# Attention scores of a cached decode kernel: queries as weights in a zeroed block, transposed keys moving, exponentials turned back on TensorE

## Chip, core and metric

The kernel runs on one core of one Trainium2 chip. The metric is the device time of one execution in microseconds (us). An execution is profiled by the hardware profiler; other executions are timed without it.

The engines are called as the profile calls them: PE is the matrix engine, whose weight loads (PEld) overlap its matmuls; DVE, ACT and POOL are the vector, scalar and general engines; SP issues the transfers (DMA). Each engine takes its instructions in order. A matmul holds one operand in the array as weights (128 x 128) and streams the other, the moving one, through it column by column into PSUM.

## What is computed

Two decoder layers with shared weights, for 8 batch elements with one new token each. A layer is grouped attention over a cache of 8192 keys and values (32 query heads, 8 key/value heads, head size 128), then an MLP, each behind a layer norm and with a residual:

```python
def _A_ref(x, k_cache, v_cache, wq, wo):
    q = (x @ wq).reshape(B, Sq, Hq, Dh).transpose(0, 2, 1, 3)
    k = jnp.repeat(k_cache, rep, axis=1)
    v = jnp.repeat(v_cache, rep, axis=1)
    scores = jnp.einsum("bhqd,bhkd->bhqk", q, k) * (Dh ** -0.5)
    p = _softmax(scores, axis=-1)
    o = jnp.einsum("bhqk,bhkd->bhqd", p, v)
    return o.transpose(0, 2, 1, 3).reshape(B, Sq, Hq * Dh) @ wo

x = x + _A_ref(_layernorm(x), k_cache, v_cache, wq, wo)
x = x + _B_ref(_layernorm(x), w1, w2)          # silu(x @ w1) @ w2
x = x + _A_ref(_layernorm(x), k_cache, v_cache, wq, wo)
x = x + _B_ref(_layernorm(x), w1, w2)
```

Inputs are bf16. Both layers read the same caches, 2 MB of keys and 2 MB of values for each element and key/value head.

## The kernel before

**Tasks and positions.** A task is one layer, one element and one key/value head: 4 query heads against 8192 keys; there are 128. A task has 64 chunks of 128 keys, in 8 positions of 8 chunks (1024 keys, half a slot). The SBUF arena has 27 slots of 512 KB, each for a granule (16 chunks) of keys or values. `make_tasks` orders the tasks: for each element the five heads whose keys will be kept, then three heads of the second layer of the element before, three heads of the first layer of the next element, and then the second layer of the five kept heads. The last 18 of an element's 32 granules of keys stay in the arena, transposed, between the layers, so those tasks load almost only values.

**The loop (L616).** For each position `p` the instructions are recorded in this order:

- `emit_t_until(p + LT)`: PE transposes the 8 key chunks of position p + 3 against `ident` into one of three PSUM banks `TPp` (L387), and DVE or ACT copies them back over the keys (L395, L393).
- `emit_s(p)`: the scores (L418). Each chunk of 128 transposed keys is the weights, and 32 columns of queries (4 wanted, the rest overwritten by the next chunk or unused) move. The scores lie as 128 keys by 64 chunks x 4 heads in a PSUM bank `SCp`.
- `emit_pv(p - LP)`: the values of the position 12 earlier (L468), again with the chunk as weights, 4 columns of exponentials moving.
- At the first four positions after a task: `softmax_max` (DVE's reduce L427, POOL's all-reduce over the partitions L429), `softmax_exp` (DVE subtracts, L436; ACT's exp, L443), `softmax_sum` (DVE's reduce L448, POOL's all-reduce L451), `softmax_rcp` (L456).
- One step of an element's chain, if one is under way. A chain is what lies between the layers: output projection, layer norm in three steps (DVE, with POOL's all-reduces L492 and L507), up, silu, down, layer norm again, queries of the second layer; 11 steps, PE's matmuls being those of L536.
- `emit_norm` (L482) where the values of a task are done; after an element's last task of the first layer its chain begins.
- `issue_until(p)`: SP's loads that have a free slot.

**Order and waits.** The loads are planned ahead (`plan_loads`): the order is that of the positions at which they are needed, `LT` ahead of the scores for keys and `LP` behind for values, each into the slot that becomes free first. Each engine has one counting semaphore; `Sync` records for each tile who wrote and read it last and makes an instruction wait for these. At L619, before the first task of the second layer of an element, what is left of its chain is recorded in one go. When the tasks are done, the projection, norm and MLP of the second layer follow for all 8 elements at once.

Of the kernel before, what the change touches and what calls it, by code (L numbers as in the profile page):

```python
# [5 lines left out]
HQ = 32  # L6
# [6 lines left out]
GRP = 8  # L13
# [3 lines left out]
KEEP = 18  # L17
LT = 3
PRE = 10
LP = 12  # L20
SW = 32
NTP = 3
NSCP = 2
NP = 3
NST = 4
ACT_EVAC = (1, 4, 7)

BF16 = mybir.dt.bfloat16
# [160 lines left out]
def _build(ctx, nc, A_x, A_k_cache, A_v_cache, A_wq, A_wo, B_w1, B_w2, out):  # L189
# [39 lines left out]
    def chunk(slot, c):  # L229
        o = slot * SLOT + c * 128  # L230
        return ARENA[:, o:o + 128]
# [7 lines left out]
    w1_sb = sb([128, KT, F], BF16, "w1")  # L239
    w2_sb = sb([128, FT, D], BF16, "w2")  # L240
    ident = sb([128, 128], BF16, "ident")
    Xr = sb([128, D], BF16, "X")
    XT = [sb([128, KT, B], BF16, f"XT{n}") for n in range(3)]
    QPAD = SW - REP
    QT1 = sb([128, B * HQ + QPAD], BF16, "QT1")
    QT2 = [sb([128, HQ + QPAD], BF16, "QT2") for _ in range(2)]
    at1 = [sb([128, HQ], BF16, "at1") for _ in range(2)]
    at2 = sb([128, HQ, B], BF16, "at2")
    vr = sb([128, B], FP32, "vr")
# [6 lines left out]
    xnT = sb([128, KT, B], BF16, "xnT")  # L256
    eh = sb([128, FT * B], FP32, "eh")
    hsT = sb([128, FT * B], BF16, "hsT")
    SCs = sb([128, NCH * REP], FP32, "SCs")
    Ps = [sb([128, NCH * REP], BF16, "P") for _ in range(NP)]  # L260
    mxp = [sb([128, REP], FP32, "mxp") for _ in range(NST)]
    mxa = [sb([128, REP], FP32, "mxa") for _ in range(NST)]
    ssm = [sb([128, REP], FP32, "ssm") for _ in range(NST)]
    ssa = [sb([128, REP], FP32, "ssa") for _ in range(NST)]
    rcp = [sb([128, REP], FP32, "rcp") for _ in range(NST)]
# [60 lines left out]
    with nc.Block() as block:  # L326

        @block.sync
        def _(sync_eng):
            dma(sp, Xr[0:B, :], x_in, wsem["x"], writes=["X"])  # L330

            op(pool, lambda: pool.memset(ident[:, :], 1.0), writes=["ident"])
            op(
# [4 lines left out]
                ),  # L338
                reads=["ident"], writes=["ident"],
            )  # L340
            op(pool, lambda: pool.memset(QT1[:, B * HQ:], 0.0), writes=["QT1"])
            for n in range(2):
                op(pool, lambda n=n: pool.memset(QT2[n][:, HQ:], 0.0), writes=[f"QT2_{n}"])

            queue = list(loads)

# [19 lines left out]
            load_rest()  # L366

            evacs = [0]
            tnext = [0]

            def has_t(i):
# [7 lines left out]
            def emit_t(i):  # L379
                b, g, k, h = where(i)  # L380
                slot = k_slot[(b, g, k)]
                n = evacs[0]
                evacs[0] += 1
                tb = n % NTP
                tpv = TPp[tb][:, :].rearrange("p (k q) -> p k q", q=128)
                steps = [
                    lambda c=c: pe.transpose(tpv[:, c, :], chunk(slot, h * GRP + c), ident[:, :])  # L387
                    for c in range(GRP)
                ]
                mm_group(steps, reads=[r_half(slot, h), "ident"], writes=[f"TP{tb}"])  # L390
                dst = half(slot, h)
                if n % 8 in ACT_EVAC:
                    op(act, lambda: act.copy(dst, TPp[tb][:, :]), reads=[f"TP{tb}"], writes=[r_half(slot, h)])  # L393
                else:
                    op(dve, lambda: dve.tensor_copy(dst, TPp[tb][:, :]), reads=[f"TP{tb}"], writes=[r_half(slot, h)])  # L395

            def emit_t_until(i):
                while tnext[0] <= min(i, NG - 1):
                    if has_t(tnext[0]):
                        emit_t(tnext[0])  # L400
                    tnext[0] += 1

            def emit_s(i):
                ti = i // GPT
                layer, _b, _g = tasks[ti]
                b, g, k, h = where(i)
                slot = k_slot[(b, g, k)]
                if layer == 0:
                    q0, qt, rq = b * HQ + g * REP, QT1, "QT1"
                else:  # L410
                    q0, qt, rq = g * REP, QT2[b % 2], f"QT2_{b % 2}"
                rhs = qt[:, q0:q0 + SW]
                bank = ti % NSCP
                steps = []
                for c in range(GRP):
                    o = ((i % GPT) * GRP + c) * REP
                    steps.append(
                        lambda c=c, o=o: pe.matmul(  # L418
                            SCp[bank][:, o:o + SW], chunk(slot, h * GRP + c), rhs, start=True, stop=True,
                        )  # L420
                    )
                mm_group(steps, reads=[r_half(slot, h), rq], writes=[f"SC{bank}"])

            def softmax_max(ti):
                bank, st = ti % NSCP, ti % NST
                scv = SCp[bank][:, 0:NCH * REP].rearrange("p (c h) -> p h c", h=REP)
                op(dve, lambda: dve.tensor_reduce(mxp[st][:, :], scv, AX.X, ALU.max),  # L427
                   reads=[f"SC{bank}"], writes=[f"mxp{st}"])
                op(pool, lambda: pool.partition_all_reduce(mxa[st][:, :], mxp[st][:, :], 128, bass.bass_isa.ReduceOp.max),  # L429
                   reads=[f"mxp{st}"], writes=[f"mxa{st}"])  # L430

            def softmax_exp(ti):
                bank, st, pb = ti % NSCP, ti % NST, ti % NP
                op(
                    dve,
                    lambda: dve.tensor_tensor(  # L436
                        SCs[:, :].rearrange("p (c h) -> p c h", h=REP),
                        SCp[bank][:, 0:NCH * REP].rearrange("p (c h) -> p c h", h=REP),
                        mxa[st][:, :].unsqueeze(1).to_broadcast([128, NCH, REP]), ALU.subtract,
                    ),  # L440
                    reads=[f"SC{bank}", f"mxa{st}"], writes=["SCs"],
                )
                op(act, lambda: act.activation(Ps[pb][:, :], SCs[:, :], ACT.Exp, scale=SM_SCALE),  # L443
                   reads=["SCs"], writes=[f"P{pb}"])

            def softmax_sum(ti):
                st, pb = ti % NST, ti % NP
                op(dve, lambda: dve.tensor_reduce(  # L448
                    ssm[st][:, :], Ps[pb][:, :].rearrange("p (c h) -> p h c", h=REP), AX.X, ALU.add),
                   reads=[f"P{pb}"], writes=[f"ssm{st}"])  # L450
                op(pool, lambda: pool.partition_all_reduce(ssa[st][:, :], ssm[st][:, :], 128, bass.bass_isa.ReduceOp.add),  # L451
                   reads=[f"ssm{st}"], writes=[f"ssa{st}"])

            def softmax_rcp(ti):
                st = ti % NST
# [2 lines left out]
            def emit_pv(i):  # L458
                ti = i // GPT
                b, g, k, h = where(i)  # L460
                slot = v_slot[(b, g, k)]
                ob, pb = ti % 2, ti % NP
                otp = OTp[ob][:, 0:REP]
                steps = []
                for c in range(GRP):
                    cc = (i % GPT) * GRP + c
                    steps.append(
                        lambda c=c, cc=cc: pe.matmul(  # L468
                            otp, chunk(slot, h * GRP + c), Ps[pb][:, cc * REP:(cc + 1) * REP],
                            start=(cc == 0), stop=(cc == NCH - 1),  # L470
                        )
                    )
                mm_group(steps, reads=[r_half(slot, h), f"P{pb}"], writes=[f"OT{ob}"])

            def emit_norm(ti):
                layer, b, g = tasks[ti]
# [109 lines left out]
            def chain_of(b):  # L586
# [13 lines left out]
                    )  # L600
                    for kt in range(KT)
                ],
                reads=["X", "ident"], writes=["MISC"],
            )
            op(dve, lambda: dve.tensor_copy(XT[0][:, :, :], MISC[:, 0:KT * B].rearrange("p (k b) -> p k b", b=B)),
               reads=["MISC"], writes=["XT0"])
            for f in ln_stages(XT[0][:, :, :], "XT0", B):
                f()
            query(B, QT1[:, 0:B * HQ].rearrange("p (b h) -> p h b", h=HQ), "QT1")()

            chain = []
            chain_b = [None]
# [1 line left out]
            ntask = len(tasks)  # L614

            for p in range(NG + LP + GPT + 1):  # L616
                if p < NG:
                    layer, b, _g = tasks[p // GPT]
                    if layer == 1 and chain and chain_b[0] == b:  # L619
                        while chain:  # L620
                            chain.pop(0)()
                emit_t_until(p + LT)
                if p < NG:
                    emit_s(p)
                if 0 <= p - LP < NG:
                    emit_pv(p - LP)
                ti, ph = p // GPT - 1, p % GPT
                if 0 <= ti < ntask and ph < 4:
                    (softmax_max, softmax_exp, softmax_sum, softmax_rcp)[ph](ti)
                if chain:  # L630
                    chain.pop(0)()
                done = p - LP - GPT
                if done >= 0 and done % GPT == 0 and done // GPT < ntask:
                    tj = done // GPT
                    emit_norm(tj)
                    layer, b, _g = tasks[tj]
                    if layer == 0 and tj == last0[b]:
                        assert not chain
                        chain.extend(chain_of(b))
                        chain_b[0] = b  # L640
                issue_until(p)
# [13 lines left out]
                ],  # L655
                reads=["XT0", "ident"], writes=["MISC"],
            )
            op(dve, lambda: dve.tensor_copy(Xr[0:B, :], MISC[0:B, :]), reads=["MISC"], writes=["X"])
            syn.acquire(sp, reads=[res("X")])
            sp.dma_start(out_v, Xr[0:B, :]).then_inc(osem, 16)  # L660
            sp.wait_ge(osem, 16)

# [27 lines left out]
```

## Time and profile before

| what | us |
|---|---|
| median of 3 runs (1325.31 to 1330.08) | 1327.78 |
| the profiled execution's own span | 1321.8 |
| PE busy, matmuls / weight loads | 1009.8 / 983.4 |
| DVE / ACT / POOL busy | 545.3 / 328.8 / 117.8 |
| key transposes L387, 5888 of 128 x 128 | 564.0 |
| scores L418, 8192 of 128 x 32 | 394.2 |
| values L468, 8192 of 128 x 4 | 361.0 |
| all-reduces of the softmax, L429 / L451, 128 each | 47.7 / 55.2 |
| DVE's L427 / L436 / L448, ACT's L443, 128 each | 53.3 / 53.8 / 53.2, 53.4 |

The DMA engines moved 473.5 MB of inputs, a mean of 361 GB/s over the span. How to read it: matmuls overlap each other, so the busy times of PE are sums of overlapping spans, and the pace is read from the starts in the timeline. In a line of the timeline, the numbers are the start and the length in us; what stands in brackets at the end is the engine's idle time before the line and what ended it, "issue" being idle time for which the profile shows no cause. A line of windows gives, for each engine, the busy time and in brackets the instructions, then the granted clock of PE (1.00 is full), the busy share of the DMA engines and GB/s. The strip cuts the span in 40 slices of 33 us; its digits are tenths.

### The profile page before, as it was taken

How to read it: one execution, taken by the hardware profiler on the slowest of the kernel's cores; microseconds unless marked ns; L12 is line 12 of the kernel's file. 1: busy time of each engine (PE TensorE's matmuls, PEld its weight loads, DVE VectorE, ACT ScalarE, POOL GpSimd, SP SyncE). 2: the span in 40 equal slices, each digit the busy share in tenths (PEclk: the TensorE clock that was granted, in tenths of full speed). 3: DMA queues.
4: the chain of work that ended last, by engine and by line, in shares of the span. 5: the costliest groups of instructions: out<-in, count | busy, mean ns of one | idle time of the engine just before them, and what ended most of it. 6: DMA issues, size and time to landing. Idle time of an engine off the chain costs nothing.

```text
span 1321.8 us, 57028 instructions
## 1 busy us (share of the span) xinstructions
PE 1009.8 (76%) x25592; PEld 983.4 (74%) x25592; DVE 545.3 (41%) x1462; ACT 328.8 (25%) x414; POOL 117.8 (9%) x301
## 2 busy tenths in 40 slices
PE   3758867878677877778778886788867787788875
PEld 3757767877677877778778786787867787788874
DVE  2424434444343533444344442454434454344432
ACT  1323113312132222322123221331313222132210
POOL 0000010000000110000100001000010011000010
PEclk7878658858688776877678675886868867677765
DMA  8999899969999799997999889997999979999892
GB/s 342 386 399 403 291 371 408 377 230 398 408 407 376 256 407 407 408 344 286 408 408 395 303 344 407 408 383 275 377 408 407 388 243 407 407 406 357 287 408 112
DMA packets 133985, 477.14 MB, mean 361 GB/s; under 512 B 14176, under 2 KB 20080, under 8 KB 133232
## 3 DMA queue, kind: packets, MB, share of 16 engines
q1 hardware_dynamic: 133744, 473.51, 92.2%
q8 instruction: 203, 3.33, 1.0%
q14 instruction: 38, 0.31, 0.1%
HBM read 473.44 MB, written 0.01 MB: 358 GB/s over the span
## 4 chain that ended last, share of the span: by engine, by line
PE 53%; DMA 23%; issue 17%; DVE 5%; SPq 1%; POOL 1%; ACT 0%; POOLq 0%; DVEq 0%; ACTq 0%
PE TPp L387 24%; DMA arena<-in_A_k_cache_dram 18%; PE SCp L418 12%; PE OTp L468 11%; PE MISC L536 7%; DMA arena<-in_A_v_cache_dram 3%; SPq L301 1%; DVE arena L395 1%; DMA wq<-in_A_wq_dram 1%; DVE yr L522 1%; DVE tr L520 1%; DVE tr L519 1%; POOL s1a L507 0%; DVE xnT L524 0%; DVE yr L514 0%
## 5 line engine op out<-in xcount | busy, mean ns | idle before, releaser
L387 PE MATMUL TPp<-ident,arena 128*128 128x128 bf16 x5888 | 564.0, 253 | 109.2 <-DMA arena<-in_A_k_cache_dram 70.8
L387 PEld LDWEIGHTS TPp<-ident,arena 128*128 128x128 bf16 x5888 | 425.2, 113 | 117.4 <-DMA arena<-in_A_k_cache_dram 78.7
L395 DVE COPY arena<-TPp 128x1024 bf16<-128x1024 bf16 x460 | 317.3, 690 | 454.7 <-PE TPp L387 452.2
L393 ACT COPY arena<-TPp 128x1024 bf16<-128x1024 bf16 x276 | 278.6, 1010 | 688.6 <-PE TPp L387 688.6
L418 PE MATMUL SCp<-QT,arena 128*128 128x32 bf16 x8192 | 394.2, 184 | 68.6 <-issue 65.6
L468 PE MATMUL OTp<-P,arena 128*128 128x4 bf16 x8192 | 361.0, 165 | 79.3 <-issue 69.7
L418 PEld LDWEIGHTS SCp<-QT,arena 128*128 128x128 bf16 x8192 | 338.8, 103 | 71.0 <-issue 67.5
L468 PEld LDWEIGHTS OTp<-P,arena 128*128 128x128 bf16 x8192 | 290.7, 100 | 91.8 <-issue 81.0
L443 ACT ACTIVATE P<-SCs 128x256 bf16<-128x256 f32 x128 | 53.4, 417 | 271.4 <-DVE SCs L436 216.6
L429 POOL PARTITION_ALL_REDUCE mxa<-mxp x128 | 47.7, 373 | 727.0 <-DVE mxp L427 722.9
L451 POOL PARTITION_ALL_REDUCE ssa<-ssm x128 | 55.2, 431 | 296.4 <-DVE ssm L448 273.9
L427 DVE TENSOR_REDUCE mxp<-SCp 128x4 f32<-128x256 f32 x128 | 53.3, 417 | 46.5 <-PE SCp L418 46.5
L436 DVE TENSOR_TENSOR SCs<-SCp,mxa 128x256 f32<-128x256 f32 x128 | 53.8, 420 | 39.7 <-POOL mxa L429 39.7
L448 DVE TENSOR_REDUCE ssm<-P 128x4 f32<-128x256 bf16 x128 | 53.2, 416 | 41.2 <-ACT P L443 41.2
L536 PE MATMUL MISC<-xnT,wq 128*128 128x1 bf16 (+1 forms) x1152 | 31.8, 165 | 18.3 <-DVE xnT L524 18.2
L536 PEld LDWEIGHTS MISC<-xnT,wq 128*128 128x128 bf16 x1152 | 31.0, 102 | 19.1 <-DVE xnT L524 13.9
L482 DVE TENSOR_TENSOR at<-OTp,rcp 128x4 bf16<-128x4 f32 x128 | 20.0, 156 | 61.0 <-PE OTp L468 61.0
L536 PE MATMUL MISC<-at,wo 128*128 128x1 bf16 (+1 forms) x1152 | 32.5, 165 | 13.0 <-issue 12.7
L536 PEld LDWEIGHTS MISC<-at,wo 128*128 128x128 bf16 x1152 | 31.4, 101 | 13.7 <-issue 13.3
L456 DVE RECIPROCAL rcp<-ssa 128x4 f32<-128x4 f32 x128 | 22.0, 172 | 22.8 <-POOL ssa L451 22.8
L536 PE MATMUL MISC<-xnT,w 128*128 128x1 bf16 (+1 forms) x504 | 14.6, 165 | 18.4 <-DVE xnT L524 18.4
L536 PEld LDWEIGHTS MISC<-xnT,w 128*128 128x128 bf16 x504 | 13.9, 102 | 19.2 <-DVE xnT L524 17.2
(36 smaller groups left out, 111.2 us busy)
## 6 DMA issues: line engine op xcount, KB each, us to landing
arena<-in_A_v_cache_dram SPq DMA_DIRECT2D x512, 512.0 KB, 10.3
arena<-in_A_k_cache_dram SPq DMA_DIRECT2D x368, 512.0 KB, 12.2
wq<-in_A_wq_dram SPq DMA_DIRECT2D x2, 2048.0 KB, 9.4
wo<-in_A_wo_dram SPq DMA_DIRECT2D x1, 4096.0 KB, 26.0
w<-in_B_w_dram SPq DMA_DIRECT2D x2, 1792.0 KB, 22.6
X<-in_A_x_dram SPq DMA_DIRECT2D x1, 8.0 KB
out_dram<-X SPq DMA_DIRECT2D x1, 8.0 KB
```

The lines of the kernel that those rows point to most:

```text
L387: lambda c=c: pe.transpose(tpv[:, c, :], chunk(slot, h * GRP + c), ident[:, :])
L393: op(act, lambda: act.copy(dst, TPp[tb][:, :]), reads=[f"TP{tb}"], writes=[r_half(slot, h)])
L395: op(dve, lambda: dve.tensor_copy(dst, TPp[tb][:, :]), reads=[f"TP{tb}"], writes=[r_half(slot, h)])
L418: lambda c=c, o=o: pe.matmul(SCp[bank][:, o:o + SW], chunk(slot, h * GRP + c), rhs, start=True, stop=True,)
L427: op(dve, lambda: dve.tensor_reduce(mxp[st][:, :], scv, AX.X, ALU.max), reads=[f"SC{bank}"], writes=[f"mxp{st}"])
L429: op(pool, lambda: pool.partition_all_reduce(mxa[st][:, :], mxp[st][:, :], 128, bass.bass_isa.ReduceOp.max), reads=[f"mxp{st}"], writes=[f ...
L436: lambda: dve.tensor_tensor(SCs[:, :].rearrange("p (c h) -> p c h", h=REP), SCp[bank][:, 0:NCH * REP].rearrange("p (c h) -> p c h", h=REP) ...
L443: op(act, lambda: act.activation(Ps[pb][:, :], SCs[:, :], ACT.Exp, scale=SM_SCALE), reads=["SCs"], writes=[f"P{pb}"])
L448: op(dve, lambda: dve.tensor_reduce(ssm[st][:, :], Ps[pb][:, :].rearrange("p (c h) -> p h c", h=REP), AX.X, ALU.add), reads=[f"P{pb}"], wr ...
L451: op(pool, lambda: pool.partition_all_reduce(ssa[st][:, :], ssm[st][:, :], 128, bass.bass_isa.ReduceOp.add), reads=[f"ssm{st}"], writes=[f ...
L468: lambda c=c, cc=cc: pe.matmul(otp, chunk(slot, h * GRP + c), Ps[pb][:, cc * REP:(cc + 1) * REP], start=(cc == 0), stop=(cc == NCH - 1),)
L536: lambda o=o, k=k: pe.matmul(MISC[:, o * n:(o + 1) * n], w_sb[:, k, o * 128:(o + 1) * 128], rhs_of(k), start=(k == 0), stop=(k == kparts - 1),
```

## The change

The scores change sides. For each task, POOL copies its 4 query columns into a zeroed tile `QB` of 143 columns, 16 columns apart (`emit_q`). Of it, a 128-column slice that begins at 15 - j is the weights for key block j: query r then stands in column 16 r + j, and the other columns are zero. 512 transposed keys move at a time, 16 matmuls accumulate in one PSUM bank, and row 16 r + j gets the scores of head r against block j; 64 rows are used. The maximum per head becomes a reduce along the row and, across the rows of a head, two 32 x 32 transposes with a small reduce and a scaling on DVE; ACT's exp reads the scores from PSUM with that as its bias and sums each row; POOL multiplies a mask `hm` (which row belongs to which head) by these sums and adds over the partitions. PE turns the exponentials back, four transposes per task (`emit_pt`), DVE copies the 64 used columns to `PT`, and the values read columns of it 16 elements apart. The tiles for the input and the exponentials are one (`P`). Queries are copied three positions ahead, so a chain is recorded to its end three positions earlier, and the values lag 14 positions.

```diff
-LP = 12
-SW = 32
+LP = 14
-NP = 3
+NPT = 2
+NQB = 2
+KB = 512
...
+    NJ = NCH * 128 // KB
+    NR = NJ * REP
+    CPB = KB // 128
+    JPG = GRP * 128 // KB
+    QB = [sb([128, NJ - 1 + 128], BF16, "QB") for _ in range(NQB)]
...
+            def emit_q(ti):
+                layer, b, g = tasks[ti]
+                if layer == 0:
+                    q, rq = QT1[:, b * HQ + g * REP:b * HQ + (g + 1) * REP], "QT1"
+                else:
+                    q, rq = QT2[b % 2][:, g * REP:(g + 1) * REP], f"QT2_{b % 2}"
+                qb = QB[ti % NQB][:, 0:REP * NJ].rearrange("p (r j) -> p r j", j=NJ)[:, :, NJ - 1]
+                op(pool, lambda: pool.tensor_copy(qb, q), reads=[rq], writes=[f"QB{ti % NQB}"])
...
-                for c in range(GRP):
-                    o = ((i % GPT) * GRP + c) * REP
+                for c in range(JPG):
+                    j = (i % GPT) * JPG + c
                     steps.append(
-                        lambda c=c, o=o: pe.matmul(
-                            SCp[bank][:, o:o + SW], chunk(slot, h * GRP + c), rhs, start=True, stop=True,
+                        lambda c=c, j=j: pe.matmul(
+                            SCp[bank][:, :], QB[qn][:, NJ - 1 - j:NJ - 1 - j + 128], keys[:, c * KB:(c + 1) * KB],
+                            start=(j == 0), stop=(j == NJ - 1),
                         )
                     )
...
             def softmax_max(ti):
+                op(dve, lambda: dve.tensor_reduce(mxa[:, 0:1], SCp[bank][0:NR, :], AX.X, ALU.max),
+                   reads=[f"SC{bank}"], writes=["mxa"])
+                op(dve, lambda: dve.transpose(mxb[:, :], mxa[:, :]), reads=["mxa"], writes=["mxb"])
+                op(dve, lambda: dve.tensor_reduce(
+                    mxh[:, :], mxb[:, :].rearrange("p (r j) -> p r j", j=NJ), AX.X, ALU.max),
+                   reads=["mxb"], writes=["mxh"])
+                op(dve, lambda: dve.tensor_scalar(
+                    mxa[:, :].rearrange("p (r j) -> p r j", j=NJ),
+                    mxh[:, :].unsqueeze(2).to_broadcast([NR, 32 // NJ, NJ]), -SM_SCALE, None, op0=ALU.mult),
+                   reads=["mxh"], writes=["mxa"])
+                op(dve, lambda: dve.transpose(mxb[:, :], mxa[:, :]), reads=["mxa"], writes=["mxb"])
...
+                op(act, lambda: act.activation(
+                    P[0:NR, :], SCp[bank][0:NR, :], ACT.Exp, bias=mxb[:, 0:1], scale=SM_SCALE, accum_out=rs[st][:, :]),
+                   reads=[f"SC{bank}", "mxb"], writes=["P", f"rs{st}"])
 
             def softmax_sum(ti):
-                op(dve, lambda: dve.tensor_reduce(
-                    ssm[st][:, :], Ps[pb][:, :].rearrange("p (c h) -> p h c", h=REP), AX.X, ALU.add),
-                   reads=[f"P{pb}"], writes=[f"ssm{st}"])
+                op(pool, lambda: pool.tensor_scalar(
+                    ssm[st][0:NR, :], hm[:, :], rs[st][:, 0:1], None, op0=ALU.mult),
+                   reads=["hm", f"rs{st}"], writes=[f"ssm{st}"])
                 op(pool, lambda: pool.partition_all_reduce(ssa[st][:, :], ssm[st][:, :], 128, bass.bass_isa.ReduceOp.add),
                    reads=[f"ssm{st}"], writes=[f"ssa{st}"])
+
+            def emit_pt(ti):
+                pb = ti % NPT
+                tb = evacs[0] % NTP
+                evacs[0] += 1
+                tpv = TPp[tb][:, 0:KB].rearrange("p (c q) -> p c q", q=128)
+                steps = [
+                    lambda c=c: pe.transpose(tpv[:, c, :], P[:, c * 128:(c + 1) * 128], ident[:, :])
+                    for c in range(CPB)
+                ]
+                mm_group(steps, reads=["P", "Pz", "ident"], writes=[f"TP{tb}"])
+                op(dve, lambda: dve.tensor_copy(PT[pb][:, :, :], tpv[:, :, 0:NR]), reads=[f"TP{tb}"], writes=[f"PT{pb}"])
...
-                            otp, chunk(slot, h * GRP + c), Ps[pb][:, cc * REP:(cc + 1) * REP],
+                            otp, chunk(slot, h * GRP + c), pv[:, cc % CPB, cc // CPB, :],
...
+            LQ, LPT = 3, 4
+            emit_q(0)
...
-                if p < NG:
-                    layer, b, _g = tasks[p // GPT]
+                tq = (p + LQ) // GPT
+                if (p + LQ) % GPT == 0 and tq < ntask:
+                    layer, b, _g = tasks[tq]
                     if layer == 1 and chain and chain_b[0] == b:
                         while chain:
                             chain.pop(0)()
+                    emit_q(tq)
...
+                if 0 <= ti < ntask and ph == LPT:
+                    emit_pt(ti)
```

In the changed kernel POOL's multiply is line L472, its all-reduce L475 and its copy of the queries L431.

## The prediction

> **What bounds the kernel now.** I read the page's strip of 40 slices first, then the windows, then PE's and POOL's timelines. The strip:
>
> ```profile
> POOL 0000010000000110000100001000010011000010
> PEclk7878658858688776877678675886868867677765
> ...
> GB/s 342 386 399 403 291 371 408 377 230 398 408 407 376 256 407 407 408 344 286 408 408 395 303 344 407 408 383 275 377 408 407 388 243 407 407 406 357 287 408 112
> ...
> q8 instruction: 203, 3.33, 1.0%
> ```
>
> The caches arrive at a ceiling of 408 GB/s, with eight dips: 473.5 MB at 408 is 1160 us of 1321.8. Each dip is one element's chain (projection, layer norms, MLP, queries), whose steps PE takes in order between tasks. A window around one has 238 GB/s for 32 us (424 to 456), so 32 x (1 - 238/408) = 13 us are lost per chain, 8 x 13 = 107 in all; start and tail are the rest. POOL is nearly idle: 117.8 us, two all-reduces per task of 371 and 431 ns.
>
> A second limit lies close by. PE's weight loads in the tasks that keep their keys (timeline of that engine):
>
> ```profile
> 334.68 0.16 PEld L418 LDWEIGHTS SCp<-QT,arena 128*128 128x128 bf16 x3
> 337.62 0.21 PEld L418 LDWEIGHTS SCp<-QT,arena 128*128 128x128 bf16 x5 [2.78 <-issue]
> ...
> 341.24 0.10 PEld L418 LDWEIGHTS SCp<-QT,arena 128*128 128x128 bf16 x1
> 344.17 0.26 PEld L418 LDWEIGHTS SCp<-QT,arena 128*128 128x128 bf16 x7 [2.83 <-issue]
> ```
>
> PE stops 2.8 us every 6.5 us with nothing to wait for. 203 instruction transfers for 51,184 PE instructions are one per 252, and 203 x 6.4 is 1300 us: PE's instructions come hardly faster than it needs them.
>
> PE's clock halves and doubles between 3.41 us windows. Transposes (first count) in four of them:
>
> ```profile
> core 0: us, PE busy (x), PEclk, DMA share, GB/s
> 428.31:431.72 3.41, 2.61 (x23) 0.50 0.28 85
> 431.72:435.13 3.41, 0.30 (x5) 1.00 1.03 386
> 435.13:438.55 3.42, 2.03 (x16) 0.50 0.45 169
> 438.55:441.96 3.41, 1.41 (x13) 0.50 0.71 251
> ```
>
> With 24 score matmuls (32 columns) and 24 value ones (4) the first streams 23 x 128 + 768 + 96 = 3808 columns, and the next window has clock 1.00; the third, 16 x 128 + 512 + 64 = 2624, is followed by 0.50. In a chain PE seldom gets enough columns for full clock.
>
> **What decides.** POOL's timeline at the start:
>
> ```profile
> 0.78 0.20 POOL L332 MEMSET ident<- 128x128 bf16 x1 [0.29 <-POOLq L675]
> 9.19 0.28 POOL L335 TENSOR_SCALAR_AFFINE_SELECT ident<-ident 128x128 bf16<-128x128 bf16 x1 [8.20 <-issue]
> 9.44 0.11 POOL L341 MEMSET QT<- 128x28 bf16 x1
> 9.50 0.16 POOL L343 MEMSET QT<- 128x28 bf16 x2
> 25.86 0.43 POOL L492 PARTITION_ALL_REDUCE s1a<-s  x1 [16.20 <-DVE s L490]
> ```
>
> L335 needs only the memset that ended at 0.98, yet starts at 9.19: 8.20 us of "issue". In the list of the built program's instructions an unnamed entry stands just ahead of L335, and one ahead of the first all-reduce (L492), where its time, at most the 16.2 us before it, is covered by DVE's wait. After that POOL runs nothing but all-reduces, and no such entry comes. So it stands where POOL goes over to another family of operations: arithmetic to all-reduce or back. The changed program's list has it 256 times more, per task: entry, L472 multiply (hm x rs), entry, L475 all-reduce, then L431 copy into QB. I take both as what L335 paid, 8.2 us.
>
> [...]
>
> **The change, part by part.**
> - POOL per task: two entries 16.4, all-reduce 0.43, and multiply and copy some 0.2 each by the memset and select rows (0.11 to 0.28), with hops 1.0 for the three: 17.4 us against 10.3 us of DMA (4.19 MB at 408). The loop closes: the scores of task t+2 need QB, whose copy is queued on POOL behind the sum of task t, so PE can't run ahead. Queued behind that copy is the next entry, so POOL never rests; two QB buffers shift this and do not shorten it.
> - PE, scores: 64 matmuls of 32 columns per task become 16 of 512. Before, a position (one half slot) at full clock goes 202.23 transpose, 202.67 scores, 202.88 values, 203.08 next: 0.85 us, scores 0.21; at half clock 1.28 (428.59 to 429.87), scores 0.26. No 512-column matmul is in the trace. From below, 16 cost no more than 64 narrow ones (0.21 per position, were width free); from above, four times the mean transpose row (253 ns) is 1.0 us each, 2.0 per position. The transposes' pace (0.42 us for 8 x 128 columns, 0.85 at half clock) is nearest: 0.43 or 0.85 per position. With the transposes back (4 per task, 0.03) a position is 1.10 or 1.92, a task 8.8 or 15.4: under POOL's 17.4 either way, so worth nothing now. Without that cover it decides (rivals).
> - PE's instructions fall from 51,184 to 39,920, so some 158 transfers, 1030 us: that limit goes, behind POOL.
> - DVE: three 0.42 us operations go; a reduce over 512 (twice the 256 of L427, 0.8), four small ones at 0.16 and a copy of PT at 0.4 come: 1.8 against 1.25 us, on an engine 41% busy. ACT: exp over 512 instead of 256, from 0.42 to 0.6 between that row and the 1024-wide copy's 1.01. POOL's cycle covers both. DMA moves the same bytes.
> - Order: values two positions later, queries three earlier. LQ flushes the chain of the first and last element (24 positions to the first kept task, of which 14 and 11 steps are 25) with five steps in a row: a few us each, under POOL too. Each chain's four all-reduces need no entry but stand ahead of one, the second a position late: 1.9 + 0.7 (evacuation) + 0.4, so 3 us, 8 times: 24.
>
> **Sum.** Queries and the first two copies at 35 us (L536 ends at 33.8, then a 1.27 us cast). First scores and exp to some 47, entry, all-reduce and copy of task 2 at 57. 125 more cycles of 17.4: 2232. Sums of the last two tasks: 35. From the last normalisation to the end 17.2 as now (1304.62 to 1321.8), chains 24: 2308. The profiled execution spans 1321.8 and the runs shown have a median of 1327.78, 6 us more; so **2315 us**.
>
> [...] I stay at 8.2 for both: it is the one bare observation, taken at 309 GB/s (window 1 to 9), between a full DMA stream and the half-loaded one to come. A quarter less or more (6.2, 10.2) gives cycles of 13.4 and 21.4: 1800 and 2820.
>
> **Rivals.** From what price does POOL decide? 2 x entry + 1.0 must exceed 10.3: from 4.6 us on. Below, DMA's 1160 us stay and the eight chains decide.
> - *Entries cost little after the first; the clock stays low in chains: 1350.* For: L492's entry shows no cost of its own. [...] Some 14 positions per chain are exposed; a half-clock position streams about 2144 columns in 1.92 us, so 3800 in a window that nothing interrupts, near the bound, and a chain's matmuls interrupt. Half of the positions at 1.92 and part at 1.10 give 1.45 against 1.28: 2.4 us x 8 = 19, the two flushes 3 each: 1347 + 6, about 1350.
> - *The same, but wide scores hold the clock up: 1308, faster.* At full clock a window of 3.41 us has room for 3 positions, 6400 columns, and keeps well over 3808 with 1.3 us lost. If the chains then run at 1.10, 14 x 0.18 = 2.5 us are won per chain, 20 in all. It decides only with entries under 4.6 us, and if the two longest interruptions (3.5 us of projection, of queries) do not halve the clock for long.
> - *The change does not free PE:* a clock that ignores wide matmuls gives 15.4 us per task and under 2000; POOL hides that too.
>
> **Numbers.** Forecast 0.91, first rival 0.05, second 0.04 (the third is inside the forecast's range). The time is the forecast's, 2315; the range 1800 to 2820 is the entry's quarter each way, which leaves the rivals and an entry outside it, some 2 in 10, out. Over 0.3%, about what a measurement here tells from no change, faster: 0.04; within: 0.01; slower: 0.95.
>
> **What will show it.** POOL's timeline: some 8 us of "issue" ahead of each L472 and each L475, 17 us from one L431 copy to the next, always. PE waits for QB at the first scores of a task, DMA falls to some 205 GB/s (473.5 MB over 2310), and PE's 6.5 us stops vanish. Wrong it would be if L472 and L475 follow their inputs within a microsecond: then the GB/s strip returns to 408 with eight dips, and the clock in these decides.

## The result and the profile after

The changed kernel takes 2344.55 us (median of 4 runs, 2340.60 to 2358.54) against 1327.19 us for the kernel before: 1.7686 times as long, with a 95% interval of 1.7631 to 1.7741. The profiled execution spans 2338.9 us. 2315 us was forecast, in a range of 1800 to 2820.

From the page of the changed kernel, first the strip of 40 slices (now 58 us each), the queue of the instruction transfers, the chain by engine, and two groups:

```profile
POOL 0000000000000000000000000000000000000000
PEclk7886678786786767868687677777778776687766
...
GB/s 363 356 182 155 232 180 163 181 226 242 198 172 157 249 245 178 193 160 269 234 169 193 199 225 252 135 201 179 239 238 151 213 194 245 207 146 189 214 219 1
...
q8 instruction: 159, 2.61, 0.4%
...
issue 63%; PE 23%; DVE 7%; POOL 4%; ACT 1%; DMA 1%; POOLq 0%; SPq 0%; ACTq 0%; DVEq 0%
...
L443 PE MATMUL SCp<-arena,QB 128*128 128x512 bf16 x2048 | 778.7, 470 | 2.0 <-POOL QB L431 1.6
```

DMA is no longer near its 408 GB/s after the second slice; the mean is 204. POOL still looks idle in the strip, because its pauses are no busy time: in the chain they stand under "issue", which is 63% of the span. The groups of POOL's instructions show them as idle time before an instruction (after the second bar):

```profile
L475 POOL PARTITION_ALL_REDUCE ssa<-ssm x128 | 56.5, 442 | 1033.9 <-issue 1033.9
L472 POOL TENSOR_SCALAR ssm<-hm,rs 64x4 f32<-64x4 f32 x128 | 38.2, 298 | 976.0 <-issue 449.0 <-ACT P L466 295.7 <-DVE arena L416 214.2
L431 POOL COPY QB<-QT 128x4 bf16<-128x4 bf16 x128 | 33.4, 261 | 20.6 <-DVE QT L619 20.6
L529 POOL PARTITION_ALL_REDUCE s1a<-s x18 | 7.2, 401 | 130.3 <-DVE s L527 106.6 <-DVE at L519 23.7
L544 POOL PARTITION_ALL_REDUCE s1a<-s x18 | 6.9, 385 | 28.4 <-DVE s L542 28.4
```

These five lines account for POOL's whole span: pauses 1033.9 + 976.0 = 2010 us, its own work for the tasks 56.5 + 38.2 + 33.4 = 128 us, and the layer norms' all-reduces with their waits, 130.3 + 28.4 + 14.1 = 173 us; with the 21 us before the copies and some 9 at the start this is 2341, against a span of 2338.9 (the copy starts 0.11 us before the all-reduce ahead of it ends). But for the waits at the layer norms and the 21 us POOL has next to no free time. Part of the idle time before L472 is put down to ACT or DVE, but the pauses with that label are not the longer ones: they have a mean of 7.4 us (40 times) and 7.1 (30), against 8.0 (56) of "issue". Two tasks in POOL's timeline:

```profile
1741.78 0.44 POOL L475 PARTITION_ALL_REDUCE ssa<-ssm  x1 [10.75 <-issue]
1742.11 0.26 POOL L431 COPY QB<-QT 128x4 bf16<-128x4 bf16 x1
1749.94 0.30 POOL L472 TENSOR_SCALAR ssm<-hm,rs 64x4 f32<-64x4 f32 x1 [7.56 <-DVE arena L416]
1759.10 0.44 POOL L475 PARTITION_ALL_REDUCE ssa<-ssm  x1 [8.86 <-issue]
1759.43 0.26 POOL L431 COPY QB<-QT 128x4 bf16<-128x4 bf16 x1
1766.82 0.30 POOL L472 TENSOR_SCALAR ssm<-hm,rs 64x4 f32<-64x4 f32 x1 [7.13 <-ACT P L466]
1773.66 0.44 POOL L475 PARTITION_ALL_REDUCE ssa<-ssm  x1 [6.55 <-issue]
```

Ahead of each multiply and of each all-reduce stand 6.5 to 10.8 us; the copy, which follows the all-reduce, has none. From one copy to the next are 17.3 us. The unnamed entries of the prediction are in the trace too, as pairs of records of POOL's sequencer (POOLq), named MODIFY_POOL_CONFIG: there are 516 such records in the changed kernel and 4 in the kernel before. In the chain a pair stands at the start of each pause, as here for the second all-reduce (start, us, what):

```profile
1750.45 0.00 POOLq L475
1750.48 0.00 POOLq L475
1750.48 8.61 issue
1759.10 0.44 POOL ssa L475
```

What POOL's lateness does to the others is in the timeline of DVE and PE just behind the first of these all-reduces:

```profile
1742.26 0.18 DVE L492 RECIPROCAL rcp<-ssa 128x4 f32<-128x4 f32 x1 [15.12 <-POOL ssa L475]
1742.35 0.26 DVE L488 COPY PT<-TPp 128x256 bf16<-128x256 bf16 x1
1742.53 0.68 DVE L416 COPY arena<-TPp 128x1024 bf16<-128x1024 bf16 x1
...
1742.76 0.36 PE L505 MATMUL OTp<-PT,arena 128*128 128x4 bf16 x8 [10.13 <-DVE PT L488]
```

DVE stood for 15.12 us at the reciprocal of the sums. Behind it in DVE's order stood the copy of the turned exponentials and an evacuation (the copy of transposed keys out of PSUM); PE's values waited 10.13 us for the first.

### The profile page after: what moved, and what is told of

It is laid out like the page before. It is cut to its first block, busy times and chain, and to the rows that moved or that the text cites. A ratio compares the mean times of both kernels' runs of the same rounds, so it can differ in the third digit from the quotient of the medians.

```text
span 2338.9 us, 46839 instructions
## 1 busy us (share of the span) xinstructions
PE 1401.9 (60%) x19960; PEld 1013.2 (43%) x19960; DVE 601.2 (26%) x1849; ACT 374.3 (16%) x542; POOL 129.4 (6%) x432
## 4 chain that ended last, share of the span: by engine, by line
issue 63%; PE 23%; DVE 7%; POOL 4%; ACT 1%; DMA 1%; POOLq 0%; SPq 0%; ACTq 0%; DVEq 0%
PE TPp L408 10%; PE SCp L443 7%; PE MISC L573 4%; PE OTp L505 3%; DVE arena L416 2%; POOL ssa L475 2%; POOL ssm L472 2%; ACT P L466 1%; DVE mxa L452 1%; ACT arena L414 1%; DVE PT L488 1%; DMA wq<-in_A_wq_dram 0%; DMA arena<-in_A_k_cache_dram 0%; DVE tr L556 0%; DVE yr L559 0%
## 5 line engine op out<-in xcount | busy, mean ns | idle before, releaser
L505 PEld LDWEIGHTS OTp<-PT,arena 128*128 128x128 bf16 x8192 | 394.1, 103 | 949.3 <-issue 761.9
L443 PE MATMUL SCp<-arena,QB 128*128 128x512 bf16 x2048 | 778.7, 470 | 2.0 <-POOL QB L431 1.6
L505 PE MATMUL OTp<-PT,arena 128*128 128x4 bf16 x8192 | 379.3, 170 | 574.9 <-DVE at L519 317.0
L408 PE MATMUL TPp<-ident,arena 128*128 128x128 bf16 x5888 | 552.9, 250 | 225.2 <-DVE arena L416 208.9
L416 DVE COPY arena<-TPp 128x1024 bf16<-128x1024 bf16 x460 | 316.1, 687 | 325.8 <-PE TPp L408 324.8
L492 DVE RECIPROCAL rcp<-ssa 128x4 f32<-128x4 f32 x128 | 22.8, 178 | 1231.0 <-POOL ssa L475 1231.0
L443 PEld LDWEIGHTS SCp<-arena,QB 128*128 128x128 bf16 x2048 | 175.9, 113 | 7.3 <-PE SCp L443 5.0
L466 ACT ACTIVATE P<-SCp,mxb 64x512 bf16<-64x512 f32 x128 | 87.2, 682 | 563.5 <-DVE mxb L462 548.8
L475 POOL PARTITION_ALL_REDUCE ssa<-ssm x128 | 56.5, 442 | 1033.9 <-issue 1033.9
L452 DVE TENSOR_REDUCE mxa<-SCp 64x1 f32<-64x512 f32 x128 | 86.8, 678 | 49.3 <-PE SCp L443 49.0
L472 POOL TENSOR_SCALAR ssm<-hm,rs 64x4 f32<-64x4 f32 x128 | 38.2, 298 | 976.0 <-issue 449.0
L484 PE MATMUL TPp<-ident,P 128*128 128x128 bf16 x512 | 50.3, 221 | 0.0
L431 POOL COPY QB<-QT 128x4 bf16<-128x4 bf16 x128 | 33.4, 261 | 20.6 <-DVE QT L619 20.6
L488 DVE COPY PT<-TPp 128x256 bf16<-128x256 bf16 x128 | 34.2, 267 | 0.0
```

Source lines behind the costliest of these rows:

```text
L443: lambda c=c, j=j: pe.matmul(SCp[bank][:, :], QB[qn][:, NJ - 1 - j:NJ - 1 - j + 128], keys[:, c * KB:(c + 1) * KB], start=(j == 0), stop=( ...
L452: op(dve, lambda: dve.tensor_reduce(mxa[:, 0:1], SCp[bank][0:NR, :], AX.X, ALU.max), reads=[f"SC{bank}"], writes=["mxa"])
L466: op(act, lambda: act.activation(P[0:NR, :], SCp[bank][0:NR, :], ACT.Exp, bias=mxb[:, 0:1], scale=SM_SCALE, accum_out=rs[st][:, :]), reads ...
L472: op(pool, lambda: pool.tensor_scalar(ssm[st][0:NR, :], hm[:, :], rs[st][:, 0:1], None, op0=ALU.mult), reads=["hm", f"rs{st}"], writes=[f" ...
L484: lambda c=c: pe.transpose(tpv[:, c, :], P[:, c * 128:(c + 1) * 128], ident[:, :])
L488: op(dve, lambda: dve.tensor_copy(PT[pb][:, :, :], tpv[:, :, 0:NR]), reads=[f"TP{tb}"], writes=[f"PT{pb}"])
```

## The experiments

Where no number of runs stands beside a time, it is that of one execution, the profiled one.

**The multiply on DVE.** One word moves one operation to another engine, and POOL keeps all-reduces and copies:

```diff
-                op(pool, lambda: pool.tensor_scalar(
+                op(dve, lambda: dve.tensor_scalar(
                     ssm[st][0:NR, :], hm[:, :], rs[st][:, 0:1], None, op0=ALU.mult),
```

> The changed kernel with the multiply hm x rs on DVE instead of POOL; POOL then runs all-reduces and the copies into QB only. Theory (POOL's going over between arithmetic and all-reduce costs some 8 us each time, twice per task, and this alone makes the change slow): the pauses ahead of POOL's all-reduces vanish and the time falls to 1300 to 1400 us, by the two rivals of the prediction 1350 (clock low in the chains) or 1308 (clock held up). Rival A (the wide scores, the way back of the exponentials or DVE's longer softmax cost much too): above 1500 us, with PE or DVE busy without a break. Rival B (the all-reduce itself is slow in this order, not the going over): no less than 2000 us.

Measured: 1334.68 us (10 runs), 1.005 times the kernel before (1.0029 to 1.0072). From its page, the strip and the chain by engine:

```profile
PEclk7889699979999799998999789998999989998796
...
GB/s 340 386 399 407 196 396 409 403 249 391 408 408 375 223 390 407 408 370 280 408 408 404 286 307 407 409 402 279 368 408 408 396 205 400 408 408 372 217 409 154
...
PE 45%; DMA 42%; DVE 7%; SPq 2%; issue 2%; POOL 0%; ACT 0%; POOLq 0%; ACTq 0%; DVEq 0%
```

The last line as it was in the kernel before:

```profile
PE 53%; DMA 23%; issue 17%; DVE 5%; SPq 1%; POOL 1%; ACT 0%; POOLq 0%; DVEq 0%; ACTq 0%
```

And the group of POOL's all-reduces, with the multiply on DVE:

```profile
L475 POOL PARTITION_ALL_REDUCE ssa<-ssm x128 | 55.6, 434 | 982.6 <-DVE ssm L472 962.5 <-PE SCp L443 9.7 <-PE TPp L408 8.3
```

The all-reduces now wait for their input, none for "issue", the trace has 4 records of MODIFY_POOL_CONFIG, and 1010 us are gone: nearly the whole loss is the change of family. What else the change does, with this multiply on DVE, costs 0.5%, between the two rivals of the prediction (1350 and 1308). The strip says why it is so little either way: DMA is back at 408 GB/s, with the eight dips of before. "Issue" fell from 17% of the chain before to 2%, and the mean clock rose from 0.739 to 0.933, yet both were limits beside DMA's, not above it.

**The multiply in the kernel before.** Its result is not used:

```diff
+                op(pool, lambda: pool.tensor_scalar(
+                    dum[0:64, :], ssm[st][0:64, :], ssm[st][0:64, 0:1], None, op0=ALU.mult),
+                   reads=[f"ssm{st}"], writes=["dum"])
                 op(pool, lambda: pool.partition_all_reduce(ssa[st][:, :], ssm[st][:, :], 128, bass.bass_isa.ReduceOp.add),
```

> The kernel before with one extra multiply of 64 x 4 elements on POOL ahead of the sum's all-reduce; its result is not used, nothing else changes. Theory: two changes of family per task, 2 x 8 us + 1.5 us of POOL's own work, and DVE's reciprocal holds back the evacuations behind it while it waits: at least 128 x 17.5 = 2240 us, up to 2850 us if the scores of a task cannot run during the wait. Rival (the cost is tied to the changed scores, not to POOL): 1330 us, the extra multiply takes 0.3 us off an idle engine.

Measured: 2557.04 us. POOL's timeline:

```profile
1000.83 0.38 POOL L431 PARTITION_ALL_REDUCE mxa<-mxp  x1 [3.11 <-DVE mxp L429]
1008.21 0.30 POOL L453 TENSOR_SCALAR dum<-ssm 64x4 f32<-64x4 f32 x1 [7.00 <-issue]
1014.77 0.44 POOL L456 PARTITION_ALL_REDUCE ssa<-ssm  x1 [6.27 <-issue]
1018.33 0.38 POOL L431 PARTITION_ALL_REDUCE mxa<-mxp  x1 [3.11 <-DVE mxp L429]
```

A task takes 17.5 us here, 20 in the mean over all 128, with nothing changed in the scores, and the trace has 516 records of MODIFY_POOL_CONFIG: the cost belongs to POOL's order. Between two all-reduces in a row (L456, L431) stands no pause, only the wait for DVE's maximum, 3.11 us.

**The multiply on POOL for every second task.**

```diff
+                eng = pool if ti % 2 else dve
+                op(eng, lambda: eng.tensor_scalar(
```

> The changed kernel with the multiply on POOL for odd tasks and on DVE for even ones: 64 multiplies on POOL instead of 128. Theory with POOL as the bound (a task pair costs POOL 2 x 8 + 2 us = 18 us against 20.6 us of DMA for keys and values, 11.4 us where only values are loaded): most is hidden, 1450 to 1700 us. Rival (each pause adds its full length to the time, hidden by nothing): halfway between the run without any and the changed kernel's 2339, some 1840 us.

Measured: 1886.89 us, near the rival's figure and not the theory's. POOL's lines and then DVE's around one pause:

```profile
1021.73 0.30 POOL L473 TENSOR_SCALAR ssm<-hm,rs 64x4 f32<-64x4 f32 x1 [8.42 <-ACT P L466]
1032.43 0.44 POOL L476 PARTITION_ALL_REDUCE ssa<-ssm  x1 [10.40 <-issue]
...
1021.80 0.69 DVE L416 COPY arena<-TPp 128x1024 bf16<-128x1024 bf16 x1 [0.40 <-PE TPp L408]
1032.90 0.18 DVE L493 RECIPROCAL rcp<-ssa 128x4 f32<-128x4 f32 x1 [10.41 <-POOL ssa L476]
```

Here the first pause lies beside the wait for the exponentials' sums, which ACT had ready 0.20 us before the multiply; in 21 of the 64 tasks the multiply follows the sums within 0.20 us, and in the others later. The second pause is passed on whole by the reciprocal. The 552 us above the kernel without multiplies on POOL are 8.6 per multiply, about the length of one pause, not of two (their means are 9.9 and 8.2). POOL's load alone does not tell the time; where its result is asked for does.

**The query copies on DVE.**

```diff
-                op(pool, lambda: pool.tensor_copy(qb, q), reads=[rq], writes=[f"QB{ti % NQB}"])
+                op(dve, lambda: dve.tensor_copy(qb, q), reads=[rq], writes=[f"QB{ti % NQB}"])
```

> The changed kernel with the copy of the queries into QB on DVE instead of POOL; the multiply stays on POOL. The prediction said that PE cannot run ahead because the scores' QB copy is queued behind POOL's sums. Theory 1 (POOL has no free time at all, whoever waits for it): only the copies' 0.26 us per task go, 2290 to 2340 us. Theory 2 (the loop over QB sets the time, POOL has free time in it): PE runs ahead, and the time falls below 2150 us.

Measured: 2331.08 us, as theory 1 has it. The loop over QB did not set the time of the changed kernel.

**The reciprocal late.** Two kernels: every second task's multiply on POOL, and every task's.

```diff
-                if 0 <= ti < ntask and ph < 4:
-                    (softmax_max, softmax_exp, softmax_sum, softmax_rcp)[ph](ti)
+                if 0 <= ti < ntask and ph < 3:
+                    (softmax_max, softmax_exp, softmax_sum)[ph](ti)
...
                     tj = done // GPT
+                    softmax_rcp(tj)
                     emit_norm(tj)
```

> The run with the multiply on POOL for every second task, with DVE's reciprocal of the sums moved from the fourth position after a task to just ahead of its normalisation, 11 positions later in DVE's order. In the run with the early one (1887 us) POOL had free time, yet each of its pauses ahead of an all-reduce was added to the time. Theory (the pause itself is exposed by the reciprocal: it stands in DVE's queue and holds back the evacuations behind it; POOL's own work of 18 us per pair fits beside the pair's 20.6 us of transfers): 1340 to 1480 us. Rival (each pause holds PE up by another way, the copies into QB): 1800 us or more.

> The changed kernel, multiply on POOL for every task, with the reciprocal moved just ahead of the normalisation. Theory (POOL is the bound by its own work: two pauses and 1.0 us per task, 16.5 to 17.4 us, whoever waits for it): 2150 to 2340 us, the reciprocal wins little. Rival (DVE's wait is the whole cause): below 1800 us.

Measured: 1569.91 us and 2201.73 us. With every task's multiply on POOL the order wins 6%: POOL's own load is the bound. Of the 139 us between the spans (2338.9 and 2200.0), 112 are waits ahead of the layer norms' all-reduces, which fell from 159 to 46 us as DVE no longer stood at the reciprocal (17.3 us in all, from 1231.0); the pauses are 1983 us against 2010. With every second it wins 317 us, but falls 90 us short of the expectation. The waits of the kernel with every task's multiply say what came in the reciprocal's place (us in total, times, longest):

```profile
POOL ssa L475 <- issue: 1008.3, 126, 10.9
...
PEld SCp L443 <- POOL QB L431: 743.1, 118, 11.6
...
PE SCp L443 <- POOL QB L431: 725.8, 114, 11.9
```

Now the scores wait for QB, 726 us in all where it had been 1.6. In the kernel with every second task's multiply the same line stands at 217.3 us.

**Both ways closed.** Every second task's multiply on POOL, late reciprocal, and the copies on DVE (the edits above together):

> The run with the multiply on POOL for every second task and the late reciprocal (1570 us, in which PE's scores wait 217 us for the copies into QB), with these copies on DVE. Theory (two ways led from POOL's pauses to PE, the reciprocal in DVE's queue and the copy queued behind the sums; with both gone POOL's 17 us per pair run beside the rest): 1335 to 1420 us. Rival (POOL's pauses slow something else too, transfers or DVE): above 1500 us.

Measured: 1449.16 us, between the theory's range and the rival's. Most of the rest went, not all: 115 us remain against the kernel without multiplies on POOL. In its waits DVE's reciprocal, though late, still waits 181.8 us for POOL, and the layer norms' all-reduces queue behind the pauses too. PE waits 65.0 us for exponentials (ACT's L466) and 40.3 for evacuations by DVE, two waits that the kernel without multiplies on POOL does not have; this points to DVE's queue again, but no run takes the 115 us apart.

**A version that beats both.** Apart from the start and the tail, the eight dips are where DMA stays below the 408 GB/s of the strips. The chain's steps come in each position; elements 1 to 6 have 48 positions until their queries are needed:

```diff
-                if chain:
+                if chain and (chain_b[0] in (0, B - 1) or p % 3 == 0):
                     chain.pop(0)()
```

Tried on the kernel with the multiply on DVE, on the kernel before, and on the first with every fourth position:

> The kernel with the multiply on DVE (1335 us), with one chain step in every third position instead of in each, for elements 1 to 6, which have 48 positions until their second layer's kept tasks; 0 and 7 stay. Theory (DMA at 408 GB/s is the bound except in the chains, where PE falls behind by its pauses; with PE's instructions no longer scarce a full-clock position takes 1.09 us against 1.285 of DMA, so three positions win back 0.6 us and the norms are ready when asked for): some 8 us less per chain, 1275 to 1300 us. Rival (PE is as busy as it can be and the chains' time is only moved): 1325 to 1335.

> The kernel before with the same spreading of the chain steps. Theory (PE's instructions come at one per 25 ns, so a position with 48 of them takes 1.2 us or, at half clock, 1.28 against DMA's 1.285, and nothing is won back between steps; only the waits for the norms go, 2 to 3 us per chain): 1300 to 1315 us. Rival (the instructions are no limit, positions at 0.85 us win back more than in the changed kernel): below 1280.

> The kernel with the multiply on DVE and the chain spread over every third position (1306 us), with every fourth instead: more room between steps, but the last step, the queries, is then recorded in one go with what is left before it. Theory (each position at full clock wins back 0.2 us, so 11 more positions win back 2 us per chain, six chains): 1290 to 1300 us. Rival (the chains' remaining loss is the long projections themselves, not their spacing): 1303 to 1312 us.

| kernel | median, us | against before (95% interval) |
|---|---|---|
| multiply on DVE, every third position | 1305.79 (4 runs) | 0.983 (0.9807 to 0.9852) |
| before, every third position | 1316.61 (4 runs) | 0.9914 (0.9890 to 0.9937) |
| multiply on DVE, every fourth position | 1318.88 (6 runs) | 0.9935 (0.9914 to 0.9955) |

The first is the fastest of the study, 29 us below the same kernel unspread; in the kernel before the same edit wins 12.5 against the runs beside it. That it wins more where PE's instructions are fewer agrees with the theory, but the clock differs as well (0.938 against 0.739), and no run separates the two; the expected 1275 to 1300 was not reached, nor quite 1300 to 1315. In the strip of the fastest:

```profile
GB/s 348 386 399 404 227 353 408 406 358 350 409 408 390 327 338 408 408 372 371 327 407 403 343 359 375 408 405 365 350 409 408 381 333 315 408 408 368 233 408 146
```

The middle six dips are wide and shallow (two or three slices at 315 to 375), and the unspread chains of elements 0 and 7 stand out at 227 and 233. Every fourth position is slower, against the expectation: what is left of a chain is then recorded in one go, and that seems to cost more than the extra room wins. The traces agree: in the chain that ends near 625 us, the second norm's two all-reduces start 1.09 us apart with every fourth position (623.13 and 624.22) and 3.66 with every third (611.00 and 614.66); and from 460 to 480 us, where another chain ends in both, DMA moves 256 GB/s against 302. How much of the 13 us this makes up is not shown.

## Why the prediction was right, and where not

- **The pause at each change of family, 16.4 us per task: right, and a little high.** 2010 us in 256 pauses are 7.85 each against 8.2, so 90 us too much. One observation stood for all: the pauses ahead of L475 go from 5.74 to 10.82 us and those ahead of L472 from 6.70 to 11.65, so that their mean lies this near is in part luck. The first-rival condition (a price under 4.6 us) was not met. Moving one operation (1334.68) and adding one to the kernel before (2557.04) show it from both sides.
- **POOL's own work, 1.0 us: right** (0.30 + 0.44 + 0.26). Of the all-reduces before, the prediction has the first at 371 ns; the page has 373, and nothing rests on it.
- **The chains, 24 us: the term that was mis-sized.** The layer norms' all-reduces took 173 us of POOL's time, 159 of it idle, of which 16 lie in the start and 9 in the tail; that leaves 17 per chain. The prediction counted 3, for one of the four in a chain. POOL's timeline at a chain has all four:

```profile
1004.38 0.40 POOL L529 PARTITION_ALL_REDUCE s1a<-s  x1 [9.39 <-DVE s L527]
1006.64 0.38 POOL L544 PARTITION_ALL_REDUCE s1a<-s  x1 [1.86 <-DVE s L542]
1017.43 0.30 POOL L472 TENSOR_SCALAR ssm<-hm,rs 64x4 f32<-64x4 f32 x1 [10.41 <-issue]
...
1029.20 0.40 POOL L529 PARTITION_ALL_REDUCE s1a<-s  x1 [4.89 <-DVE at L519]
1031.51 0.38 POOL L544 PARTITION_ALL_REDUCE s1a<-s  x1 [1.91 <-DVE s L542]
1040.95 0.30 POOL L472 TENSOR_SCALAR ssm<-hm,rs 64x4 f32<-64x4 f32 x1 [9.06 <-ACT arena L414]
```

The pause ahead of the next multiply begins only behind the two all-reduces of a norm (its records stand at 1006.97 and 1031.84 us). What the prediction left out is that DVE itself is late, as it stands at its reciprocal: with the reciprocal late in DVE's order (the kernel of 2201.73 us) the 159 us fell to 46. This term, some 110 us too small, and the pauses' excess of 90 nearly cancel, which is luck, and is why 2315 lies so near 2344.55.

- **"PE can't run ahead because the scores need QB": wrong as to where PE stands, right as to the time.** PE's scores waited 1.6 us for QB. PE stood at the values (317.0 us for DVE's normalisation L519, 256.3 for its copy L488) and at the transposes (208.9 for its evacuations L416), all of them in DVE's queue, and DVE stood 1231.0 us at its reciprocal, which the prediction had not named among what waits for POOL. The late reciprocal brings the QB wait out (726 us), so the loop was there, behind the other. As POOL was full, neither set much of the time (2331.08 with the copies moved, 2201.73 with the reciprocal moved); with half the pauses they did (1886.89, 1569.91, 1449.16).
- **Wide scores at 0.43 or 0.85 us, positions of 1.10 or 1.92: right.** In the changed kernel's timeline of PE, transposes start 1.92 us apart at a granted clock of 0.50 and 1.09 at 1.00:

```profile
1742.98 1.01 PE L408 MATMUL TPp<-ident,arena 128*128 128x128 bf16 x8
...
1744.90 1.01 PE L408 MATMUL TPp<-ident,arena 128*128 128x128 bf16 x8
...
1747.66 0.61 PE L408 MATMUL TPp<-ident,arena 128*128 128x128 bf16 x8
...
1748.75 0.61 PE L408 MATMUL TPp<-ident,arena 128*128 128x128 bf16 x8
```

DVE's reduce L452 takes 0.678 us (0.8 in the prediction) and ACT's exp 0.682 (0.6): little of the path, as said.

- **PE's instruction transfers, some 158: 159.** "Issue" fell to 2% of the chain with the multiply on DVE, and that gained nothing by itself (1334.68 us), since DMA's limit stood as high (408 GB/s in the strip of that kernel).
- **The rivals, if the pauses were cheap: 1350 and 1308.** The kernel with the multiply on DVE shows that case: 1334.68, between them. The clock did rise with the wide scores (0.933), as the second said; the chains still lost at least as much as before, as the first said: the eight dips of the strip go down to 196 to 286 GB/s there, and to 230 to 303 in the kernel before.

## What to carry to other kernels

Read the built order of an engine for what the source does not say: here one small operation of another kind between two all-reduces cost two pauses, 7.85 us each in the mean, in a strip that shows the engine as idle. A late result cost here what stood behind the first instruction that asked for it (DVE stood 1231.0 us at its reciprocal), so put the asking late in the queue: it won 317 us with every second multiply on POOL, but only 6% with every one, where the late engine itself was full. And the limit of PE's instructions ("issue", from 17% of the chain to 2%), removed beside DMA's of the same height, won nothing by itself (1334.68 us against 1327.19); here the time to win lay in the chains, where the work was slower than both limits.

## What had not been expected of the hardware

In the changed kernel the pause differs with its direction and with the traffic: with transfers at rest, at the end (2 GB/s from 2292 to 2310 us), 5.97 and 5.98 us going to the all-reduce (those at 2303.21 and 2317.01) and 7.08 to 7.30 going to the multiply, and 9.44 going to the all-reduce with 376 GB/s moving (46.1 to 55.5). Over the whole trace, with the traffic taken from the end of the multiply to the start of the all-reduce, the 8 pauses ahead of L475 in which under 50 GB/s moved are 5.81 to 6.12 us; the 36 with 250 to 300 GB/s have a mean of 9.27, from 7.54 to 10.82, and the 37 with more a mean of 8.86, from 6.34 to 10.78, so the amount of traffic alone does not set them. The pause also ran beside a wait for inputs: in the kernel before, the pair of records ahead of the first all-reduce stands at 9.9 us, and the all-reduce starts at 25.86, 0.14 us after its input. The copy into QB, though neither all-reduce nor the multiply's kind, has no pause behind an all-reduce (L431 in the timeline above).
